# Attention in front of a mixture-of-experts stack: planes and first weights made inside attention's plan, tilings of TensorE grouped, memory matrices loaded in four batches

## Chip, cores and metric

The kernel runs on one core of one Trainium2 chip. The metric is the device time of one execution in microseconds (us); smaller is better. Values are the median of several executions, and one further execution was recorded by the hardware profiler.

## The reference

Attention over 4 batches, 8 heads, 576 positions, 64 channels, with a linear memory beside it; then a mixture of 8 experts with a balanced gate; then a feed-forward layer.

```python
scores = np.where(causal, -1e9, scale * q @ k.T); a = softmax(scores); local = a @ v
q_p = phi(q); mem_out = (q_p @ M_prev) / (q_p . z_prev + 1e-6)     # phi: elu + 1
x = g * mem_out + (1 - g) * local                                   # g: sigmoid of beta, per head
P = exp(x @ w_gate - max); 8 rounds: rows of P to 1, columns of P to N / E
x = sum over e of P[:, e] * (relu(x @ w1[e]) @ w2[e])               # 2304 x 512, hidden 1024
out = g2(x @ w_in) @ w_out                                          # hidden 2048
```

## The kernel before, in words

**Two plans.** The order of the work on every engine is written by a list scheduler (`Plan`). Each operation has a kind, an engine, an estimated cost and a priority; `Plan.order` walks through a simulated time, gives each free engine the ready operation with the smallest priority, and the instructions are issued in that order, so that every engine runs its own queue strictly in it. In the first plan (attention) the priority is the pair's number plus an offset of the operation's kind (`AHEAD`); in the second (experts and feed-forward) it is a due time alone. All operations of the first plan are issued ahead of all of the second.

**Attention** works on 16 pairs of heads (`pair(p)`, 4 pairs in a batch). SP loads q, k, v and z. TensorE turns q and k (`Tq0`, `Tq1`, `Tk0`, `Tk1`; `Tk1`, line 339, turns k's last 64 positions as a 64-row operand). ACT and DVE split them into a rounded high part and a low part. The scores `S0` to `S3` (line 411) use the array as two 64-row halves, one for each head, and `S4` (line 447) is full size. DVE takes the row minima (`mn`, line 415), ACT the exponentials (`ex`, line 421), POOL the scaling (`no`, line 470). TensorE turns the weights (`A0` to `A4`, line 291), ACT and DVE copy them (`at`, lines 491 and 504) into `bat`, of which there is one buffer. Then TensorE adds up in one PSUM buffer the memory's part `me` (lines 520 and 521, on `mblk`, the memory matrices of all 16 pairs), and the values' parts `av0` to `av3` (lines 532 and 534), two 64-column halves of the array, and `avt` (line 544), 64 by 64 quarters. `xh` copies the sum to `xa` (lines 556 to 561). The memory branch is `m0a` to `m0h`, `M1`, `qt`; its `m0b` (line 359) is a one-operation pass on POOL. `mblk` is filled by two DMAs (line 1002) that are issued when the fourth z load has been.

**The gate's logits** of finished batches (`g0`, line 892) are operations of the first plan for 13 of 18 blocks; the last 5 blocks and the eight rounds (`g1` to `g8`, lines 892 to 956) belong to the second.

**Experts and feed-forward** run in 60 units of about 31 us. A unit's first products (lines 802 to 804) take the planes of a superblock of 768 tokens: seven combinations of blocks of `xa`, each split into high and low (`add_planes`: `xt` on DVE, line 727; high on ACT, line 735; low on DVE, line 736), and w1's seven combinations (`add_weights`: `ws` on POOL, line 631; lines 642 and 644). The second products are lines 840 to 842. All 14 planes and the weights of the first unit are made by operations of the second plan.

Of the kernel before, what the change touches and what calls it, by code (L numbers as in the profile page):

```python
# [9 lines left out]
F32 = mybir.dt.float32  # L10
# [56 lines left out]
class Plan:  # L67
# [6 lines left out]
    AHEAD = {"ldq": -2.5, "ldk": -2.5, "ldv": 0.606644, "ldz": -0.0188182, "dupq": 2.5, "dupk": -1.11634, "Tq0": -0.582609, "Tq1": 0.34955, "Tk0": -0.348844, "Tk1": -0.811355, "Tt": -0.756224, "xqh": 1.14314, "xql": -1.02368, "kh": -2.48941, "kl": 2.5, "xqht": 0.447842, "kht": -2.5, "xqlt": -2.31585, "klt": -2.17001, "m0a": -2.28731, "m0b": 0.537231, "m0c": 0.387496, "m0d": 0.0204494, "m0e": 2.5, "m0f": -1.69614, "m0g": -2.5, "m0h": -2.5, "M1": 1.28311, "M1t": -2.5, "qt": 0.255714, "qtt": 0.106151, "S0": -2.5, "mn0": -0.618995, "ex0": -0.690281, "S1": 0.300177, "mn1": 0.479532, "ex1": 1.23372, "S2": 0.320698, "mn2": 1.81199, "ex2": -1.35932, "S3": -1.28738, "mn3": -1.07555, "ex3": 0.927263, "S4": -0.414386, "mn4": -0.748203, "ex4": 2.5, "rs0": -0.939336, "no0": -2.5, "no1": 1.07992, "no2": 1.36276, "no3": -1.05966, "no4": 1.36881, "A0": -0.654903, "at0": -1.24412, "A1": 0.733921, "at1": 0.715315, "A2": 1.22899, "at2": 2.07211, "A3": 0.131368, "at3": 1.10354, "A4": 1.48159, "at4": -1.63997, "A4t": -0.147975, "at4t": 2.5, "me": 1.67645, "av0": -1.11291, "av1": -0.469304, "av2": 0.199915, "av3": -0.505524, "avt": -0.468038, "xh": 0.600085, "xl": -1.65062, "g0": 1.02324, "g1": -0.814666, "g2": -1.20931, "g3": 0.801005}  # L74
# [36 lines left out]

    def prio(self, x):
        return (x.p if self.strict else x.p + self.AHEAD.get(x.kind, 0.0), x.n)

    def order(self):
# [9 lines left out]
        slots = {r: r.free for r in self.rings}  # L125
        if self.strict:
            self.queue()
        while len(out) < len(self.ops):
            if not events:
                raise RuntimeError(str([(round(x.p), x.kind, [(b.ring.name, b.slot, b.may(x)) for b in x.bufs]) for e in engines for x in sorted(todo[e], key=self.prio)[:6]]))  # L130
# [8 lines left out]
            for e in engines:  # L139
# [19 lines left out]
                x.start = t  # L159
                free[e] = t + x.cost  # L160
# [4 lines left out]
                for y in x.then:  # L165
                    y.wait -= 1
                    y.ready = max(y.ready, t + x.cost + (x.lat or (self.LATENCY[e] if y.eng != e else 0.13 if e == "DVE" else 0.033)))
                    if not y.wait:
                        todo[y.eng].append(y)
                        heapq.heappush(events, y.ready)  # L170
        self.length = max(free.values())
# [4 lines left out]
def tile_attn_moe_ffn(  # L176
# [53 lines left out]

    att = ExitStack()
# [10 lines left out]
    qe = acon.tile([P, 2, P], F32, name="qe")  # L242
    mblk = acon.tile([P, B * NPAIR, P], F32, name="mblk")
# [18 lines left out]
    r_ke = ring(qk, [TAIL, 2, D], F32, "ke", 2)  # L262
# [30 lines left out]
    def pair(p):  # L293
# [5 lines left out]
        for nm, buf, src in (("q", bq, q), ("k", bk, k), ("v", bv, v)):  # L299
# [7 lines left out]
            if nm == "k":  # L307
                o("ld" + nm, "SP", 0.18, lambda s_=s_: nc.sync.dma_start(
                    out=bke(), in_=s_[:, SM:S, :].rearrange("h s d -> s h d")), wr=[(bke, 0)])
# [21 lines left out]
        for nm, buf, e_, ps in (("q", bq, bqe, bpq), ("k", bk, bke, bpk)):  # L331
# [3 lines left out]
            def turn_tail(e_=e_, ps=ps, nm=nm):  # L335
                if nm == "q":
                    transposes(ps()[:, SM:], [e_()])
                else:
# [3 lines left out]
            o(f"T{nm}1", "PE", 0.15, turn_tail, rd=[(e_, 0)] + ([(e_, 1)] if nm == "q" else []), wr=[(ps, 1)])  # L342
        mq, tq = slice(0, SM), slice(SM, S)
        whole = [(bpq, 0), (bpq, 1)]
        o("xqh", "ACT", 0.6, lambda: nc.scalar.activation(bqh(), bpq()[:, 0 : SM + P], AF.Copy, scale=-SCALE),
          rd=whole, wr=[(bqh, 0)])
        o("xql", "DVE", 0.75, lambda: nc.vector.scalar_tensor_tensor(
# [3 lines left out]
        o("kh", "ACT", 0.55, lambda: nc.scalar.copy(bkh(), bpk()[:, 0:S]), rd=whole, wr=[(bkh, 0)])  # L351
        o("kl", "DVE", 0.68, lambda: nc.vector.tensor_tensor(
# [5 lines left out]
        o("m0a", "ACT", 0.57, lambda: nc.scalar.activation(be(), bq(), AF.Exp), rd=raw, wr=[(be, 0)])  # L358
        o("m0b", "POOL", 0.68, lambda: nc.gpsimd.tensor_scalar(
            out=be(), in0=be(), scalar1=1.0, scalar2=None, op0=ALU.min), wr=[(be, 0)])  # L360
        o("m0c", "DVE", 0.8, lambda: nc.vector.scalar_tensor_tensor(
# [11 lines left out]
        o("m0d", "POOL", 1.51, zmul, rd=[(bqp, 0), (bzr, 0), (bzt, 0)], wr=[(be, 0)])  # L373
        o("m0e", "DVE", 0.67, lambda: nc.vector.tensor_reduce(out=br(), in_=be(), axis=AX.X, op=ALU.add),
          rd=[(be, 0)], wr=[(br, 0)])
        o("m0f", "DVE", 0.08, lambda: nc.vector.scalar_tensor_tensor(
            out=br(), in0=br(), scalar=1e-6, in1=d9[:, hp, :], op0=ALU.add, op1=ALU.mult), wr=[(br, 0)])
        o("m0g", "DVE", 0.13, lambda: nc.vector.reciprocal(out=br(), in_=br()), wr=[(br, 0)])
# [8 lines left out]
        o("m0h", "POOL", 1.33, scale_phi, rd=[(br, 0)], wr=[(bqp, 0)])  # L387
# [7 lines left out]
        o("qt", "ACT", 0.48, lambda: nc.scalar.copy(bqt()[:, mq], pm()[:, 0:SM]), rd=[(pm, 0)], wr=[(bqt, 0)])  # L395
# [563 lines left out]
    with tc.manual_schedule():  # L959
# [25 lines left out]
        for p in range(NP):  # L985
            pair(p)
# [9 lines left out]
        for n, x in enumerate(order):  # L996
# [10 lines left out]
            if n == free:  # L1007
                early.close()
# [74 lines left out]
```

## Time and profile before

| | us |
|---|---|
| median of 3 executions | 2176.34 (2176.3 to 2178.87) |
| profiled execution | 2174.11 |
| its span, first to last instruction | 2172.3 |

The page gives for each engine the busy time, and the work that ended last. Windows give the same for stretches of time; their columns are start and end, length, busy time and instructions of PE, PEld, DVE, ACT and POOL, the granted clock of TensorE as a share of 2.4 GHz (1.00 is 2.4 GHz, 0.50 is 1.2 GHz), the DMA engines' busy share, and GB/s. A timeline lists instructions of one engine in order: start, length, line and operation, and in brackets the idle time before it and what ended it; neighbouring ones of one kind stand in one line with their count. A group by shape has, behind its count, the busy time, the mean of one in ns, and the idle time before them. On TensorE instructions overlap, so that what a line takes is read from its start to the start of the next line.

### The profile page before, as it was taken

Reading aid. Unit: us, or ns where it says so; the run is one execution under the profiler, and the core shown is the slowest. Engines: PE = TensorE matmul, PEld = TensorE weight load, DVE = VectorE, ACT = ScalarE, POOL = GpSimd, SP = SyncE. Lnnn points to the kernel's source line nnn. Section 1 sums busy time; section 2 is a strip of 40 time slices with the busy share of each in tenths; the row PEclk is TensorE's granted clock in tenths of the full one; section 3 lists DMA queues with packets and bytes.
Section 4 is the critical chain, followed back from the end, with each engine's and each line's share of the span. In section 5 each row is a group of like instructions: output and inputs, shape, how many; then the busy total and the mean of one; then the engine's idle time right before and its main releaser. Section 6 shows DMA issues by size and latency. Waiting matters only on the chain.

```text
span 2172.3 us, 31537 instructions
## 1 busy us (share of the span) xinstructions
PE 2141.2 (99%) x11163; PEld 1875.6 (86%) x11163; DVE 1579.1 (73%) x2882; ACT 1135.9 (52%) x2785; POOL 903.3 (42%) x967
## 2 busy tenths in 40 slices
PE   6999989999999999999999999999999999999999
PEld 4666689989898989999898989899999989898988
DVE  5766599887865688887655588885555587898985
ACT  5776554444444554444444454444444456777773
POOL 4867454443433334343433343343334334344340
PEclk8999989999999999999999999999999999999999
DMA  4323123332322223333222223322212212122211
GB/s 94 81 65 70 45 68 97 107 112 97 95 86 69 69 75 110 106 111 90 83 69 69 68 83 97 103 87 69 77 59 68 68 62 75 56 100 73 98 64 39
DMA packets 165054, 174.56 MB, mean 80 GB/s; under 512 B 70432, under 2 KB 121632, under 8 KB 164896
## 3 DMA queue, kind: packets, MB, share of 16 engines
q1 hardware_dynamic: 164752, 172.54, 26.4%
q8 instruction: 88, 1.44, 0.3%
q14 instruction: 70, 0.57, 0.1%
q10 hardware_dynamic: 144, 0.00, 0.0%
HBM read 159.40 MB, written 13.11 MB: 79 GB/s over the span
## 4 chain that ended last, share of the span: by engine, by line
PE 97%; DVE 1%; DMA 1%; SPq 1%; issue 0%; POOL 0%; ACT 0%; DVEq 0%; POOLq 0%
PE py L841 15%; PE py L842 15%; PE py L840 15%; PE ph L804 13%; PE ph L803 13%; PE ph L802 13%; PE s L291 4%; PE s L534 2%; PE s L411 2%; PE s L447 1%; PE s L521 1%; PE s L892 1%; PE pk L882 0%; PE pk L892 0%; PE s L520 0%
## 5 line engine op out<-in xcount | busy, mean ns | idle before, releaser
L644 POOL TENSOR_TENSOR w1l<-ws,w1h 128x512 fp32r<-128x512 f32 x240 | 326.9, 1380 | 1022.2 <-ACT w1h L642 1022.1
L804 PE MATMUL ph<-xh,w1l 128*128 128x384 f32 x1680 | 568.0, 338 | 1.5 <-POOL w1l L644 1.5
L803 PE MATMUL ph<-xl,w1h 128*128 128x384 f32 x1680 | 567.7, 338 | 0.0
L802 PE MATMUL ph<-xh,w1h 128*128 128x384 f32 x1680 | 564.9, 336 | 0.6 <-ACT pt L783 0.6
L842 PE MATMUL py<-w2h,hl 128*128 128x512 f32 x1440 | 565.4, 393 | 0.0
L841 PE MATMUL py<-w2l,hh 128*128 128x512 f32 x1440 | 565.0, 392 | 0.0
L840 PE MATMUL py<-w2h,hh 128*128 128x512 f32 x1440 | 562.2, 390 | 0.0
L783 ACT COPY pt<-ph 128x384 f32<-128x384 f32 x480 | 230.1, 480 | 541.4 <-PE ph L804 495.4
L788 DVE TENSOR_TENSOR hx<-ph,pt 128x384 f32<-128x384 f32 x480 | 264.1, 553 | 217.7 <-PE ph L804 121.3
L802 PEld LDWEIGHTS ph<-xh,w1h 128*128 128x128 f32 x1680 | 316.4, 188 | 21.1 <-ACT pt L783 1.1
L803 PEld LDWEIGHTS ph<-xl,w1h 128*128 128x128 f32 x1680 | 315.9, 188 | 20.0
L842 PEld LDWEIGHTS py<-w2h,hl 128*128 128x128 f32 x1440 | 270.0, 187 | 57.3
L804 PEld LDWEIGHTS ph<-xh,w1l 128*128 128x128 f32 x1680 | 316.4, 188 | 2.3 <-POOL w1l L644 2.0
L841 PEld LDWEIGHTS py<-w2l,hh 128*128 128x128 f32 x1440 | 270.3, 188 | 40.7
L840 PEld LDWEIGHTS py<-w2h,hh 128*128 128x128 f32 x1440 | 270.5, 188 | 40.1
L762 ACT ACTIVATE hh<-hx 128x384 fp32r<-128x384 f32 x384 | 192.7, 525 | 196.5 <-DVE hx L788 196.2
L866 DVE SCALAR_TENSOR_TENSOR xa<-py,pg,xa 128x512 f32<-128x512 f32 x264 | 191.4, 748 | 131.0 <-PE py L842 129.1
L763 DVE SCALAR_TENSOR_TENSOR hl<-hx,hh 128x384 fp32r<-128x384 f32 x384 | 218.5, 588 | 74.3 <-ACT hh L762 72.3
L631 POOL TENSOR_TENSOR ws<-wr 128x256 f32<-128x256 f32 x240 | 199.8, 853 | 100.7 <-DMA wr<-in_moe_w_dram 87.1
L642 ACT CAST w1h<-wr 128x256 fp32r<-128x256 f32 x360 | 132.9, 403 | 89.2 <-PE ph L803 88.8
L661 DVE TENSOR_TENSOR w2l<-wr,w2h 128x512 fp32r<-128x512 f32 x240 | 165.3, 723 | 5.3 <-ACT w2h L660 5.3
L642 ACT CAST w1h<-ws 128x256 fp32r<-128x256 f32 x480 | 162.8, 405 | 0.0
(143 smaller groups left out, 2330.5 us busy)
## 6 DMA issues: line engine op xcount, KB each, us to landing
wr<-in_moe_w_dram SPq DMA_DIRECT2D x192, 512.0 KB, 3.6
wr<-wk SPq DMA_DIRECT2D x48, 512.0 KB, 3.3
cr<-in_moe_w_in_dram SPq DMA_DIRECT2D x16, 512.0 KB
wk<-xt SPq DMA_DIRECT2D x32, 256.0 KB, 4.6
cr<-in_moe_w_out_dram SPq DMA_DIRECT2D x16, 512.0 KB
out_dram<-xa SPq DMA_DIRECT2D x18, 256.0 KB, 2.0
q<-in_q_dram SPq DMA_DIRECT2D x32, 128.0 KB, 2.7
k<-in_k_dram SPq DMA_DIRECT2D x32, 128.0 KB, 2.9
```

The costliest lines, as they stand in the source:

```text
L631: o(p, "ws", "POOL", 0.8, lambda: nc.gpsimd.tensor_tensor(out=st()[:, k], in0=in0(), in1=in1(), op=op), [(raw, 0)] + [(st, i) for i in rd] ...
L642: o(p, "w1h", "ACT", 0.42, lambda k=k: nc.scalar.copy(hi()[:, k], x(k)), rd, [(hi, k)])
L644: o(p, "w1l", "DVE" if eng is nc.vector else "POOL", cost, lambda: eng.tensor_tensor(out=lo()[:, i:j], in0=x(slice(i, j)), in1=f32(hi()[:, ...
L763: o(p, "hl", "DVE", 0.75, lambda: nc.vector.scalar_tensor_tensor(out=r(), in0=x(), scalar=0.0, in1=f32(a()), op0=ALU.max, op1=ALU.subtract ...
L783: o(p, "pt", "ACT", 0.49, lambda t=part[name], s=bank[b]: nc.scalar.copy(t(), s()[:, :TH]), [(bank[b], 0)], [(part[name], 0)])
L788: o(p, "hx", "DVE", 0.56, lambda s=bank[b], t=part[name]: nc.vector.tensor_tensor(out=x(), in0=s()[:, :TH], in1=t(), op=ALU.add), [(bank[b ...
L802: nc.tensor.matmul(out_, lhsT=wh, rhs=xhi()[:, kk], start=fresh and kk == 0, stop=False, **more)
L803: nc.tensor.matmul(out_, lhsT=wh, rhs=xlo()[:, kk], start=False, stop=False, **more)
L804: nc.tensor.matmul(out_, lhsT=wl, rhs=xhi()[:, kk], start=False, stop=kk == 1, **more)
L840: nc.tensor.matmul(py(), lhsT=a()[:, ts_], rhs=hi()[:, j, :], start=f == 0, stop=False)
L841: nc.tensor.matmul(py(), lhsT=a()[:, ts_], rhs=lo()[:, j, :], start=False, stop=False)
L842: nc.tensor.matmul(py(), lhsT=r()[:, ts_], rhs=hi()[:, j, :], start=False, stop=f == 3)
```

## The change

- Priorities and costs of the first plan are new numbers throughout. The plan now adds 0.1 us on TensorE where the tiling differs from that of the operation before (`TILING`, `CHANGE`).
- `Tk1` turns a zero-padded 128 x 128 tile (`ke`) at full size. `S0` and `S1` are one operation into one PSUM buffer. `av0` to `av3` and `avt` are one operation, which waits for all copies of the turned weights. An `A` operation now holds `bat`, so that it is not planned before the pair ahead has let go of it.
- `m0b` gets a second operation (times 1). `at1` goes from ACT to DVE in odd pairs.
- `mblk` is loaded in four batches of two DMAs, one batch behind each of the first four z loads.
- The planes of the first superblock and w1 of the first unit's first half are operations of the first plan, with a priority behind that of pair 15 (before its kinds' offsets). Their high parts are made on POOL instead of ACT. The planes wait for the first 8 pairs; the weights' load waits for the last use of q's and k's buffers, where their memory is.
- The pools of the second plan are opened in two steps for that; w1's two buffers lie in two pools.

```diff
+    TILING = {"S0": 1, "S1": 1, "S2": 1, "S3": 1, "av0": 2, ..., "avt": 3}
+    CHANGE, SAME = 0.1, 0.0
...
-                    nc.tensor.transpose(ps()[:, SM:S], e_().rearrange("p h d -> p (h d)"), ident[0:TAIL, 0:TAIL])
+                transposes(ps()[:, SM:], [e_()])
...
-            out=be(), in0=be(), scalar1=1.0, scalar2=None, op0=ALU.min), wr=[(be, 0)])
+            out=be(), in0=be(), scalar1=1.0, scalar2=1.0, op0=ALU.min, op1=ALU.mult), wr=[(be, 0)])
...
+            ps, c = (first, 2 * P * i) if i < 2 else (r_s.new(), 0)
+            if i != 1:
+                def rows_of(ps=ps, i=i, w=w):
+                    for j, c, n in ((0, 0, 2 * P), (1, 2 * P, 2 * P)) if i == 0 else ((i, 0, w),):
+                        scores([halves(ps())[:, h, c : c + n] for h in range(2)], slice(P * j, P * (j + 1)), 0, n)
...
-                  rd=[(ba[i], h)], wr=[(pt, h)])
+                  rd=[(ba[i], h)], wr=[(pt, h), (bat, 8 + 2 * i + h)])
...
-            o(f"av{j}", "PE", [1.02, 0.78, 0.56, 0.35][j], local,
-              rd=vs + [(bat, i) for i in range(j, NQ + 1)], wr=[(bpo, 0)])
+        o("av0", "PE", 2.86, all_local,
+          rd=vs + [(bat, i) for i in range(NQ + 1)] + [(bat4, 0), (bat4, 1)], wr=[(bpo, 0)])
...
+                    o(p, "bh", "POOL", 0.7, lambda k=k: copy1(v4(hi())[:, k], x()[:, k]), xk + rd, [(hi, k)])
...
+        def low(p, *a, **k):
+            return op(NP - 0.5 + 0.01 * p, *a, **k)
+        early_rings = (r_q, r_k, r_qh, r_ql, r_kh, r_kl)
+        add_planes(low, 0, 0, [(keys[p], 0) for p in range(NPAIR * -(-SB // S))])
+        add_weights(low, 0, 0, 1, 0, [x for x in plan.ops if any(b.ring in early_rings for b in x.bufs)])
...
-                if nz == 4:
+                if nz <= B:
                     for h in range(2):
+                        r = slice(D * h, D * (h + 1))
                         nc.sync.dma_start(
-                            out=mblk[D * h : D * (h + 1), :, D * h : D * (h + 1)],
-                            in_=M_prev.rearrange("b (hp h) d e -> h d (b hp) e", h=2)[h],
+                            out=mblk[r, NPAIR * (nz - 1) : NPAIR * nz, r],
+                            in_=M_prev[nz - 1].rearrange("(hp h) d e -> h d hp e", h=2)[h],
...
-        add_planes(o, 0, 0)
-        for g in range(2):
-            add_weights(o, 0, g, 1, GROUP * 2 * g)
+        add_weights(o, 0, 1, 1, GROUP * 2)
```

## Rows read from the trace of the kernel before

**Rows 1.** The page, part 1: busy time, share of the span, instructions.

```profile
PE 2141.2 (99%) x11163; PEld 1875.6 (86%) x11163; DVE 1579.1 (73%) x2882; ACT 1135.9 (52%) x2785; POOL 903.3 (42%) x967
```

**Rows 2.** Windows of a stall, a pair, attention's end and the rest.

```profile
40.00:47.00 7.00, 3.40 (x11) 2.31 (x11) 0.46 (x1) 0.00 (x0) 0.00 (x0) 0.53 0.47 90
104.80:118.30 13.50, 13.50 (x99) 8.78 (x98) 9.93 (x32) 10.57 (x28) 10.82 (x16) 1.00 0.34 77
265.50:293.30 27.80, 20.99 (x98) 18.90 (x96) 23.39 (x48) 16.52 (x43) 14.98 (x12) 0.69 0.12 39
293.30:2172.30 1879.00, 1875.29 (x9398) 1694.14 (x9397) 1389.42 (x2317) 947.86 (x2295) 714.62 (x704) 1.00 0.26 82
```

**Rows 3.** Waits of PE, whole span: total, times, longest.

```profile
PE s L520 <- DMA mblk<-in_M_prev_dram: 8.7, 1, 8.7
PE pk L949 <- DVE cs L947: 2.6, 1, 2.6
```

**Rows 4.** Timelines of SP, DVE and ACT between 38 and 48.

```profile
38.49 1.35 SPq L1002 DMA_DIRECT2D mblk<-in_M_prev_dram  x2
...
46.54 0.96 DVE L491 COPY at<-s 128x768 f32<-128x768 f32 x1 [10.12 <-PE s L291]
...
47.08 0.59 ACT L504 COPY at<-s 128x512 f32<-128x512 f32 x1 [10.76 <-PE s L291]
```

**Rows 5.** Timeline of PE, 104.5 to 118.6, one pair's period.

```profile
105.30 0.50 PE L411 MATMUL s<-kh,qh 64*128 64x512 f32 x2
105.64 0.40 PE L411 MATMUL s<-kl,qh 64*128 64x512 f32 x2
105.88 0.39 PE L411 MATMUL s<-kh,ql 64*128 64x512 f32 x2
106.20 0.66 PE L291 MATMUL s<-ident,a 128*128 128x128 f32 x4
...
111.33 0.60 PE L291 MATMUL s<-ident,k 128*128 128x128 f32 x4
111.76 0.27 PE L291 MATMUL s<-ident,qe 128*128 128x128 f32 x1
111.97 0.27 PE L339 MATMUL s<-ident,ke 64*128 64x64 f32 x1
112.17 0.49 PE L520 MATMUL s<-qt,mblk 128*128 128x128 f32 x2
...
115.16 0.97 PE L534 MATMUL s<-at,v 128*64 128x448 f32 x4
116.07 0.33 PE L291 MATMUL s<-ident,qp 128*128 128x128 f32 x1
116.32 0.76 PE L534 MATMUL s<-at,v 128*64 128x320 f32 x4
117.01 0.39 PE L411 MATMUL s<-kh,qh 64*128 64x256 f32 x2
```

**Rows 6.** POOL's groups, 104.8 to 118.3; the last row is the page's.

```profile
L359 POOL TENSOR_SCALAR e<-e 128x576 f32<-128x576 f32 x1 | 1.6, 1648 | 0.0
L470 POOL TENSOR_SCALAR a<-a,rs,o 128x384 f32<-128x384 f32 x2 | 1.3, 662 | 0.0
...
L644 POOL TENSOR_TENSOR w1l<-ws,w1h 128x512 fp32r<-128x512 f32 x240 | 326.9, 1380 | 1022.2 <-ACT w1h L642 1022.1
```

**Rows 7.** Timeline of PE: the gate's two longest runs, ahead of and behind attention's end.

```profile
141.62 3.74 PE L892 MATMUL s<-gw_raw,xa 128*128 128x8 f32 x32
...
266.37 6.84 PE L892 MATMUL pk<-gw_raw,xa 128*128 128x8 f32 x40 [0.83 <-ACT xa L559]
```

**Rows 8.** Window behind the third run of logits, same columns as group 2.

```profile
254.80:261.60 6.80, 6.80 (x33) 6.80 (x34) 0.58 (x2) 2.09 (x3) 3.96 (x7) 0.50 0.00 1
```

**Rows 9.** Groups by shape, DVE, 262 to 290: busy, mean ns, idle.

```profile
L727 DVE TENSOR_TENSOR xt<-xa,xt 128x384 f32<-128x384 f32 x4 | 3.8, 998 | 0.0
L727 DVE TENSOR_TENSOR xt<-xa 128x384 f32<-128x384 f32 x4 | 2.1, 550 | 0.0
```

More of the change, by code (lines that the diff above doesn't have):

```diff
@@ L110, in queue @@
                     line.append(b)
+    TILING = {"S0": 1, "S1": 1, "S2": 1, "S3": 1, "av0": 2, "av1": 2, "av2": 2, "av3": 2, "avt": 3}
+    CHANGE, SAME = 0.1, 0.0
     def prio(self, x):
-        return (x.p if self.strict else x.p + self.AHEAD.get(x.kind, 0.0), x.n)
+        same = x.eng == "PE" and self.TILING.get(x.kind, 0) == self.tiling
+        return (x.p if self.strict else x.p + self.AHEAD.get(x.kind, 0.0) - self.SAME * same, x.n)
     def order(self):
@@ L125, in order @@
         slots = {r: r.free for r in self.rings}
+        self.tiling = 0
         if self.strict:
@@ L159, in order @@
                 x.start = t
+                if e == "PE":
+                    x.cost += self.CHANGE * (self.TILING.get(x.kind, 0) != self.tiling)
+                    self.tiling = self.TILING.get(x.kind, 0)
                 free[e] = t + x.cost
@@ L170, in order @@
                         heapq.heappush(events, y.ready)
+        for _, _, x in ends:
+            for b in x.bufs:
+                b.left -= 1
         self.length = max(free.values())
@@ L261, in tile_attn_moe_ffn @@
     r_qe = Ring(lambda: qe[:, next(turns_) % 2], 2)
-    r_ke = ring(qk, [TAIL, 2, D], F32, "ke", 2)
+    tails_ = iter(range(2 * NP))
+    r_ke = Ring(lambda: ke[:, next(tails_) % 2], 2)
     r_v = ring(io, [P, NG, D], F32, "v", 3)
@@ L460, in recip @@
                 nc.vector.reciprocal(out=x, in_=x)
-            o(f"rs{g0}", "DVE", 0.3, recip, rd=[(bsm, g) for g in range(g0, g1)], wr=[(brs, g0)])
+            o(f"rs{g0}", "DVE", 0.6, recip, rd=[(bsm, g) for g in range(g0, g1)], wr=[(brs, g0)])
         for j in range(NQ + 1):
@@ L494, in pair @@
             both_ = slice(0, 2)
-            if i == 2:
-                o(f"at{i}", "DVE", (2 * n * P + 62) * 1.042e-3, lambda move=move: move(nc.vector.tensor_copy, both_),
+            if i == 2 or i == 1 and p % 2:
+                o(f"at{i}", "DVE", 0.96 if i == 2 else 0.7, lambda move=move: move(nc.vector.tensor_copy, both_),
                   rd=[(pt, 0), (pt, 1)], wr=[(bat, i)])
             else:
-                o(f"at{i}", "ACT", 2 * n * P * 0.833e-3 + 0.06, lambda move=move: move(nc.scalar.copy, both_),
+                o(f"at{i}", "ACT", (0.37, 0.59, 0.8, 1.0)[i], lambda move=move: move(nc.scalar.copy, both_),
                   rd=[(pt, 0), (pt, 1)], wr=[(bat, i)])
@@ L721, in add_planes @@
         v4 = lambda t: t.rearrange("p k (i t) -> p k i t", t=P)
-        xk = [(kx[i0 + i], 0) for i in range(2 * HT)]
+        xk0 = [(kx[i0 + i], 0) for i in range(2 * HT)]
+        xk = xk or xk0
         def tmp(in0, in1, op, rd, p):
@@ L986, in tile_attn_moe_ffn, with open_pool @@
             pair(p)
+        def open_pool(name):
+            bufs = {"s": 2, "ph": 4, "py": 3}.get(name, 1)
+            space = {"d": bass.MemoryType.DRAM, "ph": PSUM, "py": PSUM, "pk": PSUM}.get(name)
+            more = {} if space is None else dict(space=space)
+            if space is not bass.MemoryType.DRAM:
+                more["reuse_waits"] = "tile"
+            pools[name] = ctx.enter_context(tc.tile_pool(name=f"m_{name}", bufs=bufs, **more))
         for j in range(B - 1):
```

113 lines of the change are left out of this document (60 added, 53 removed).

## Prediction

> **What bounds the kernel now.** I read the page's busy times first, then windows by stage, then the waits of PE, then the timelines of the stretches that stood out. PE is busy for 99% of the span [rows 1], which says little by itself: matmuls overlap, and the same work takes twice as long where the clock is granted at 0.50. The windows say more [rows 2]. From 293.30 to the end PE has 1875.29 us of work in 1879.00 us at clock 1.00. None of that work changes, so these 1879 us stay. What can move is the 293 us ahead of them, in three places. The start has a stall: PE waited 8.7 us, in one piece, for `mblk` [rows 3]. The middle is dense: a pair takes 13.50 us and PE is busy for 13.50 of them at clock 1.00, while POOL has 10.82, ACT 10.57 and DVE 9.93 [rows 2]. Attention's end is thin: 27.80 us at a mean clock of 0.69 [rows 2].
>
> **First change: the memory matrices in batches.** The two `mblk` DMAs were issued at 38.49 and took 1.35 us of SP [rows 4]. DVE then stood idle for 10.12 us and ACT for 10.76 us [rows 4], and POOL did nothing from 40 to 47 [rows 2]. So all three had run as far ahead as they could, and nothing else is late next: without this wait all of them move up. The clock was also low there: 0.53 from 40 to 47, of which PE worked 3.40 us [rows 2], or 1.7 us at the full clock. The first batch goes out behind the first z load, and `me` of pair 0 needs no other. Gain: at most 8.7 + 1.7 = 10.4. Against it, eight DMAs instead of two: at 1.35 / 2 = 0.68 us each [rows 4], six more hold SP 4.1 us longer at the start, and the loads of pairs 1 to 3 are queued behind them, with TensorE's turns waiting for those. If all of it counts, 6.3 are left. A first pair that is late for another reason would leave none of it. I take 9, nearer the upper end, because the engines idled through the whole wait; range 0 to 10.4.
>
> **Second change: fewer tilings.** In the pair from 104.8 to 118.3 I count 16 changes of tiling on PE: three visits to the scores' row halves, one of `Tk1`, four of `av`, one of `avt`. A change is priced by what it adds to neighbours of the same shape. Four turns in a row take 111.76 - 111.33 = 0.43, so 0.11 each; a single turn between two tilings takes 116.32 - 116.07 = 0.25 [rows 5]. That is 0.14 on the neighbour's side of a visit. The visit itself adds more: `av` takes 0.91 for 448 columns (115.16 to 116.07) and 0.69 for 320 (116.32 to 117.01) [rows 5]. The slope is 0.22 for 128 columns, which leaves 0.91 - 448 x 0.00172 = 0.14 that doesn't depend on columns. So each `av` visit that goes is worth 0.14 to 0.28. Four of five go: 0.56 to 1.12. I take 0.8, the middle, because part of the fixed 0.14 may be loads of new weights that stay. `Tk1`: the turn ahead of it takes 111.97 - 111.76 = 0.21, itself 0.20 [rows 5], and at full size both would take 0.11; `me` behind it pays again. That is 0.2 to 0.3; I take 0.25. A visit of the scores: S3's takes 106.20 - 105.30 = 0.90, its steps in stream 0.24 (105.64 to 105.88), three of them 0.72, so 0.18, and 0.14 beside it: 0.32 [rows 5]. There are three visits now, and the merged S0 and S1 allow three or fewer. The gain is 0 to 0.65; I take 0.15, near the lower end, because `SAME` is 0 and nothing but the new priorities brings the visits together. Sum for a pair: 0.8 + 0.25 + 0.15 = 1.2 (0.76 to 2.07). From the end of the stall, 47, to 265.5 there are 218.5 us. In them lie 104 matmuls of the gate's logits, by my count, at 3.74 / 32 = 0.117 each [rows 7], 12.2 us, and some 7 us that the clock at 0.50 beside them costs; 199 us are left, 14.5 pairs. 1.2 x 14.5 = 17.4. A period of 12.3 is nearer to the other engines' times, so some waits of PE come back. I take off 2.4 and keep 15, range 4 to 28.
>
> That cover has to hold. POOL's one-operation pass takes 1648 ns on 576 columns, a two-operation one 662 ns on 384 [rows 6], so at most about 1.0 on 576, and POOL falls from 10.82 to about 10.2. `at1` has 512 columns, 0.59 on ACT, and some 0.7 on DVE, where 768 take 0.96 [rows 4]; in every other pair it changes over, which leaves ACT at 10.3 and DVE at 10.3. The merged `av` waits for `avt`'s copies too, and while PE runs it (some 3 us) the turns and scores of the next pair are queued behind it, with ACT and DVE behind those; they have work of the pairs on either side. I cost that at nothing; if their cover is gone, it is inside the 2.4.
>
> **Third change: planes and first weights inside attention.** Behind attention's last `avt` PE needs: 40 logits matmuls, which took 6.84 where the clock was mostly 0.50 and would take 3.74 x 40 / 32 = 4.7 at the full clock [rows 7]; 48 products of 384 columns until 293.3, by my count, at 0.18 each where 512 columns take 0.24 [rows 5], 8.6; about 0.5 for the rounds. That is 13.8 of 27.8 [rows 2], so 14 are lost: half clock and waits for planes, weights and rounds. With planes and weights ready, products follow the logits at once. What stays: 0.83 until `xa` is there, 6.84 - 4.7 = 2.1 for the slow logits [rows 7], 1 to 3 until the dense products have the clock back (half of 2 to 6 us; a slow stretch here lasts 6.8 [rows 8]), and waits for the rounds of 0 to 2.6, which is what one such wait cost [rows 3]. That is 4 to 8.6, so the gain is 5.4 to 10. I take 8.
>
> What is moved costs other engines work in the second half of attention. DVE: 8 `xt` and 14 low parts of 550 ns [rows 9], 12.1 us. POOL: 14 high parts at the 662 ns of the same width [rows 6], 9.3, and of the first weights two low parts at 1380 [rows 6] and four combinations of half that width, about 5.5. ACT: seven casts of 256 columns, about 3 by 0.59 for 512 [rows 4]. Over the last 8 pairs POOL gets 14.8 / 8 = 1.9 more for each: 10.2 + 1.9 = 12.1 beside PE's 12.3. At that load it is hidden, but barely. It has priority behind pair 15 before offsets, so what doesn't fit waits for the gaps that the gate's logits leave.
>
> Two engines on one memory show too: `xt` with two inputs took 550 ns while POOL was idle and 998 ns on average while POOL was at work [rows 9]. The Trainium skill (GPSIMD Engine Reference, section 1, Specifications) says that POOL shares its SBUF interface with VectorE and that DVE instructions with two SBUF inputs contend with it. By this, high parts on POOL beside low parts on DVE would take nearly twice as long.
>
> **Sum.** 9 + 15 + 8 = 32. The profiled execution, 2174.11 with a span of 2172.3 and 1.8 around it, would become 2142. It lies 2.2 below the median of 2176.34; I take the difference from the median: 2144. The ends of the terms give 0 + 4 + 5.4 = 9.4 (2167) and 10.4 + 28 + 10 = 48.4 (2128).
>
> **Rivals.** *Another engine bounds the pairs.* POOL at 12.1, slowed by DVE at its side, holds the second half of attention at 13.5. For: the sum above, and 998 against 550 ns [rows 9]. Against: POOL is idle beside the gate's logits, and all its added work can wait. Then only the first 6.5 pairs gain: 9 + 7.8 + 8 = 25, 2151; if the whole of attention stays at 13.5, 2159. *The change does not do what it says at one end.* Either batches queue up in front of q and k, so that the first pair is as late as now (32 - 9, 2153), or low-priority planes are left over at attention's end, so that the thin stretch stays (32 - 8, 2152). For: the planes come last in the order, and SP issues almost without pause at the start. Against: `mblk` is 5 us behind everything else, and half of attention is time enough for 12 us of DVE. *Slower: the clock falls inside the pairs.* With the scores together and `av` in one run, what is left between them is long runs of turns alone. Where PE ran the rest of some logits and then turns (254.80 to 261.60), it was busy for 6.80 of 6.80 and the clock stood at 0.50 [rows 8]. Each us at 0.50 loses half a us. Half such a stretch in each pair, 3.4, costs 1.7 x 14.5 = 25: 2169. A whole one costs 49: 2193. It turns the sign once 32 x 2 = 64 us, or 4.4 us of each pair, run at 0.50. Against: a pair already has runs of turns and is at 1.00 throughout [rows 2]. The Trainium skill (TensorE: Matmul & The Clock Gate, Part 4) says that transposes don't count as busy for the clock in the way that matmuls do; by that rule this is what grouping would bring, and the trace agrees with it only where logits stood beside the turns.
>
> **How the numbers follow.** The forecast, all three terms at about these sizes: 0.60, at 2144, with 2128 to 2160 of its own. Another engine as bound: 0.16, at 2151 to 2159. One end that doesn't gain: 0.10, at about 2152. The clock inside the pairs: 0.09, a third of it near 2169, a third near now, a third slower. Something that I don't see: 0.05, most of it slower. The range of 2127 to 2163 holds the forecast nearly whole and the next two, and leaves out the clock's cases and the tails. About 0.2% (4.4 us) is what a measurement of this kernel can tell from no change. Faster by more: 0.60 + 0.16 + 0.10 + 0.03 = 0.89; within it 0.03 + 0.01 = 0.04; slower 0.03 + 0.04 = 0.07.
>
> **What would show it.** Right: no wait of PE for `mblk` over 1 us, and the first `avt` near 43 instead of 52.7; some 8 to 10 tiling changes in a pair, and a period near 12.3 with PE dense at 1.00; products right behind the last logits, and the dense stage beginning about 19 us after the last `avt` instead of 28. Wrong: PE waits for POOL or ACT inside pairs, clock 0.50 away from the logits, `xt` still running on DVE behind attention, or a dense stage that is longer than 1879.

## The result, and the profile after

The changed kernel takes 2141.42 us (median of 4 runs, 2140.47 to 2144.26) against 2176.32 (4 runs), a ratio of 0.9841 with a 95% interval of 0.9824 to 0.9858. Its profiled execution took 2140.47, with a span of 2138.7; the span is 33.6 shorter than that of before, 2172.3. The forecast was 2144, so the total and the sign came out. The three terms behind the total did so less well: two were too small, and the first was too large. What the first one named, the batches, brought nothing that shows in the new order (e3 below). That the total is so close is in part luck.

To see this, the span is cut at marks that all the kernels have: the `avt` of the first, the second and the last pair, read from PE's timelines. At the first `avt` both kernels have the same work behind them: 173 matmuls in the trace of after, 174 in that of before. At the second they have not (264 and 250), because the two orders divide the pairs differently. So before and after are compared from the first `avt`. The experiments that keep the order of after can be compared with it from the second one, too. The column "at 0.50" adds up the stretches between the second and the last `avt` in which the granted clock was 0.50; about half of it is the time that this cost, since PE is busy there. The kernels e1 to e12 are the experiments below; their marks are those of one execution each.

| kernel | median us | first `avt` at | second `avt` at | from there to the last `avt` | of it at 0.50 | last `avt` to the end |
|---|---|---|---|---|---|---|
| before | 2176.32 | 52.7 | 63.3 | 201.9 | 13.7 | 1907.1 |
| after | 2141.42 | 47.6 | 60.5 | 181.5 | 10.2 | 1896.7 |
| e1 tile_pad | 2156.42 | 48.5 | 62.2 | 195.8 | 17.1 | 1898.3 |
| e2 tile_mix | 2169.21 | 49.3 | 63.8 | 204.9 | 13.7 | 1899.9 |
| e3 mblk_one | 2143.15 | 46.5 | 59.0 | 183.3 | 10.2 | 1899.6 |
| e4 both_late | 2149.13 | 47.0 | 61.1 | 182.6 | 17.1 | 1905.3 |
| e5 old_batches | 2172.17 | 44.9 | 58.0 | 204.6 | 20.5 | 1909.4 |
| e6 planes_late | 2149.45 | 47.2 | 61.3 | 182.7 | 17.1 | 1903.5 |
| e7 pool_twice | 2166.03 | 50.1 | 64.9 | 201.1 | 20.5 | 1898.2 |
| e8 start_pool_one | 2145.20 | 49.2 | 62.0 | 184.9 | 17.1 | 1896.5 |
| e9 k_first | 2163.08 | 46.6 | 61.8 | 201.5 | 23.9 | 1898.2 |
| e10 k_first_pool_one | 2158.51 | 45.8 | 61.0 | 199.0 | 20.5 | 1896.7 |
| e11 k_all | 2171.59 | 60.4 | 75.3 | 197.0 | 17.1 | 1896.6 |
| e12 pool_one | 2142.51 | 47.4 | 60.2 | 188.0 | 23.9 | 1896.7 |

From before to after: -5.1 up to the first `avt`, -18.1 over the 15 pairs from there to the last one, -10.4 from the last `avt` on. Forecast were -9, -15 and -8. In neither kernel does time at 0.50 lie between the first and the second `avt`.

The kernel before was timed again beside the experiments. Its medians were 2178.22 beside e1 to e4, 2177.27 beside e5 to e8, 2179.42 beside e9 to e11 and 2178.34 beside e12. So a difference of 1 to 3 us between a run and after, which was timed beside a median of 2176.32, says nothing by itself.

The page's busy time (part 1) of after stands beside [rows 1]: PE has 27.4 us less at the same count of instructions, so most of the gain is matmuls that take less time, not waits that went. Not all of that is tilings: in these two executions the clock was at 0.50 for 47.8 us of before and 28.4 us of after.

```profile
PE 2113.8 (99%) x11163; PEld 1876.2 (88%) x11163; DVE 1578.7 (74%) x2891; ACT 1125.7 (53%) x2763; POOL 917.6 (43%) x981
```

Windows of after, columns as in [rows 2]: the stretch of the old stall, two pairs one after the other, a run of turns inside a pair, attention's end up to the 48th product, and the rest.

```profile
40.00:47.00 7.00, 6.71 (x52) 4.43 (x54) 6.13 (x26) 6.41 (x20) 6.89 (x10) 1.00 0.40 85
...
85.40:97.60 12.20, 12.20 (x101) 8.96 (x99) 9.78 (x31) 10.14 (x27) 10.00 (x14) 1.00 0.40 92
97.60:109.90 12.30, 12.30 (x100) 9.04 (x98) 11.04 (x33) 10.65 (x29) 12.00 (x17) 1.00 0.34 78
113.86:116.63 2.77, 2.77 (x26) 2.60 (x25) 2.61 (x8) 2.40 (x6) 2.22 (x2) 1.00 0.40 97
242.00:259.90 17.90, 16.56 (x102) 15.56 (x101) 8.78 (x19) 8.87 (x23) 8.41 (x10) 0.90 0.31 108
259.90:2138.66 1878.76, 1874.83 (x9397) 1693.89 (x9396) 1386.71 (x2324) 946.67 (x2293) 714.30 (x705) 1.00 0.26 82
```

Beside [rows 2]: a pair takes 12.2 to 12.3 in place of 13.5, PE dense in both. Attention's end takes 17.90 at 0.90 in place of 27.80 at 0.69. The rest is 1878.76 against 1879.00: the same, as it should be. The old stall's stretch is full of work. What is not seen there is where the stall went. The waits of PE in after, beside [rows 3] (total, times, longest):

```profile
PE s L305 <- DMA k<-in_k_dram: 7.7, 2, 6.5
PE s L305 <- DMA q<-in_q_dram: 5.2, 2, 4.5
PE s L305 <- POOL a L485: 4.6, 3, 3.9
PE py L877 <- DVE hl L798: 1.3, 1, 1.3
```

The wait of 8.7 for `mblk` is gone, and two others, 6.5 for `k` and 3.9 for POOL's `a`, stand ahead of the first pair. PE's timeline shows them, and where the first pair's memory product now lies (L535):

```profile
23.90 1.08 PE L305 MATMUL s<-ident,k 128*128 128x128 f32 x4 [6.50 <-DMA k<-in_k_dram]
...
32.54 0.91 PE L305 MATMUL s<-ident,a 128*128 128x128 f32 x2 [3.88 <-POOL a L485]
...
43.66 0.39 PE L535 MATMUL s<-qt,mblk 128*128 128x128 f32 x2
...
44.84 0.45 PE L548 MATMUL s<-at,v 128*64 128x128 f32 x4
45.11 2.54 PE L550 MATMUL s<-at,v 128*64 128x448 f32 x16
47.58 0.33 PE L565 MATMUL s<-at,v 64*64 64x64 f32 x4
```

The product starts at 43.66. In the kernel before it started at 43.60, released by the load.

### The profile page after: what moved, and what is told of

It reads as the page before. It is cut to its first block, busy times and chain, and to the rows that moved or that the text cites. A ratio compares the mean times of both kernels' runs of the same rounds, so it can differ in the third digit from the quotient of the medians.

```text
span 2138.7 us, 31548 instructions
## 1 busy us (share of the span) xinstructions
PE 2113.8 (99%) x11163; PEld 1876.2 (88%) x11163; DVE 1578.7 (74%) x2891; ACT 1125.7 (53%) x2763; POOL 917.6 (43%) x981
## 4 chain that ended last, share of the span: by engine, by line
PE 97%; DVE 1%; SPq 1%; POOL 1%; issue 0%; DMA 0%; ACT 0%; DVEq 0%; POOLq 0%; ACTq 0%
PE py L876 16%; PE py L877 15%; PE py L875 15%; PE ph L839 14%; PE ph L838 14%; PE ph L837 14%; PE s L305 3%; PE s L550 2%; PE s L422 2%; PE s L927 1%; PE s L536 1%; PE s L462 1%; PE pk L917 0%; POOL a L485 0%; SPq L316 0%
## 5 line engine op out<-in xcount | busy, mean ns | idle before, releaser
L797 ACT ACTIVATE hh<-hx 128x384 fp32r<-128x384 f32 x384 | 192.8, 525 | 188.2 <-DVE hx L823 188.0
L662 POOL TENSOR_TENSOR ws<-wr 128x256 f32<-128x256 f32 x240 | 199.0, 850 | 100.7 <-DMA wr<-in_moe_w_dram 87.0
```

The source lines that it names most:

```text
L662: o(p, "ws", "POOL", 0.8, lambda: nc.gpsimd.tensor_tensor(out=st()[:, k], in0=in0(), in1=in1(), op=op), [(raw, 0)] + [(st, i) for i in rd] ...
```

## Experiments

### Is the tiling change itself what a pair saves?

A pair of before has 16 changes of tiling, one of after 7. The visits of `av` shrink from four to one, and two of the three visits of the scores now lie next to `av` or `avt`. PE's timeline of after, the seven lines of one pair at which the tiling changes:

```profile
110.20 0.39 PE L422 MATMUL s<-kh,qh 64*128 64x256 f32 x2
...
111.11 1.97 PE L305 MATMUL s<-ident,a 128*128 128x128 f32 x16
...
116.63 0.50 PE L422 MATMUL s<-kh,qh 64*128 64x512 f32 x2
...
117.53 0.49 PE L535 MATMUL s<-qt,mblk 128*128 128x128 f32 x2
...
118.70 0.44 PE L422 MATMUL s<-kh,qh 64*128 64x384 f32 x2
...
119.42 0.45 PE L548 MATMUL s<-at,v 128*64 128x128 f32 x4
...
122.16 0.33 PE L565 MATMUL s<-at,v 64*64 64x64 f32 x4
```

Two kernels put changes back while the work stays equal. Both add four small full-size products in each pair, which add products with zeros. e1 has them in one place, ahead of `av`; e2 has one behind each product of `av`. They differ in the number of changes alone: 116 against 215 in all of attention, where after has 103 and before 255. (e1 has 13 more than after, because its full-size products part the scores from `av`; "no tiling changes" in its expectation is not quite so.)

```
 def all_local():                        # e1
+    for f in locals_:
+        nc.tensor.matmul(bpo()[:, c0 + P : c0 + P + 8], lhsT=mask[:, 0:P], rhs=ident[:, 0:8], start=False, stop=False)
     for f in locals_:
         f()

 def all_local():                        # e2
     for f in locals_:
         f()
+        nc.tensor.matmul(bpo()[:, c0 + P : c0 + P + 8], lhsT=mask[:, 0:P], rhs=ident[:, 0:8], start=False, stop=False)
```

> The changed kernel with four small extra matmuls (full-size weights of zeros, 8 columns, added to the sum) in every pair, all four ahead of the values' first product, so that no tiling changes. Each is two passes like the gate's logits, 0.117 a pass: 4 x 0.23 = 0.94 us for a pair, 15 us for 16 pairs. Both theories: 2141 + 15 = 2156.

> The same four extra matmuls, one behind each of the values' four products, so that four visits to the half tiling stand where one was; the order of everything else is the same. Theory (a change of tiling costs PE time by itself): over the kernel with the four in front, 4 visits x 0.25 to 0.28 = 1.0 to 1.1 us for a pair, 16 to 18 in all: about 2173. Rival (the pairs became shorter by the new order and costs, not by tilings): the same as with the four in front, 2156.

Measured: 2156.42 and 2169.21. The 99 changes cost 12.8 us, 0.13 each. The stretch between the marks says the same: with half of the time at 0.50 taken off, 195.8 - 8.5 = 187.3 and 204.9 - 6.8 = 198.1, so 10.8 for the 86 changes that lie there, 0.13. PE's timeline of one pair of e2:

```profile
115.61 0.93 PE L550 MATMUL s<-at,v 128*64 128x448 f32 x4
116.47 0.39 PE L559 MATMUL s<-ident,mask 128*128 128x8 f32 x2
116.78 0.97 PE L550 MATMUL s<-at,v 128*64 128x448 f32 x4
```

A small product holds PE for 0.31 here (116.47 to 116.78), and `av`'s product ahead of it for 0.86 (115.61 to 116.47). In e1 the four small ones stand in one row of eight that takes 1.06, 0.26 for two. So only a part of a change is seen on the small one, and the rest on its neighbour. 9 changes fewer in a pair at 0.13 give 1.2, and the period fell by 1.25. The expectation for e2 was too high by its count: it added four visits of 0.25 to 0.28 to a pair, where the edit adds three (from one to four). Two changes at 0.13 are 0.26, so the price of a visit was right. That the changes would be free is ruled out. The Trainium skill (TensorEngine Tiling (Array Packing), Tiling Modes, Key Properties) says that a switch of the tiling mode drains TensorE. It gives no price; these two runs do.

### Were the batches worth 9?

e3 is the kernel after with one load of all memory matrices behind the fourth z load, where before had it. e5 is the kernel before with the batches and nothing else.

```
-                if nz <= B:                    # e3
-                    ... mblk[r, NPAIR * (nz - 1) : NPAIR * nz, r] <- M_prev[nz - 1]
+                if nz == B:
+                    ... mblk[D * h : D * (h + 1), :, D * h : D * (h + 1)] <- M_prev
```

> The changed kernel with the memory matrices loaded at once behind the fourth z load, as before; all else and its order unchanged. Theory A (in the new order the first product with them stands no earlier on PE than before, at 43.7 us, and waits for nothing): the one load is issued at about 37 to 38 and lands by 42 to 43, PE waits under 1 us for it, and the time is 2141 within 2. Rival, as predicted (the batches are what took the wait away): PE waits 4 to 8 us for it and the time is 2145 to 2150.

> The kernel before with one thing of the change: the memory matrices in four batches, one behind each of the first four z loads. Theory A (in the old order PE stood still for that load alone, as the prediction has it): the wait of 8.7 us goes, the first avt comes 8 to 10 us earlier, 2166 to 2169. Theory B (the next thing in the queues, a load that SP issues later because of the batches, takes its place as it did in the changed kernel): 2 to 5 us, 2171 to 2174.

e3 took 2143.15 (2139.84 to 2144.15), 1.7 more than after, with the runs of both overlapping. Its second `avt` even came sooner, at 59.0. In the new order PE gets to the product at 42.47, and the one load has landed by then. It gave that back: 1.8 were lost between the second and the last `avt` and 2.9 behind the last `avt`, where 10.2 us at 0.50 stood in place of 3.4, and its span is 3.2 longer than after's. Against the kernel before that was timed beside it e3 is 35.1 faster, and after is 34.9 faster against its own. So in the new order the batches bring nothing that these runs can show.

In the old order they do: e5 took 2172.17 (10 runs) against 2177.27, a ratio of 0.9974 (0.9964 to 0.9983), about 5 us. PE's timeline of e5 shows the product at 33.92 without a wait, and the first `avt` at 44.94, where before had it at 52.66:

```profile
33.92 0.44 PE L520 MATMUL s<-qt,mblk 128*128 128x128 f32 x2
...
44.94 0.48 PE L544 MATMUL s<-at,v 64*64 64x64 f32 x4
```

So 7.7 were gained at the first `avt`, which is close to the 9. But the second `avt` came only 5.4 sooner (57.97 against 63.34): in the kernel before the second pair followed the first by 10.7, in e5 by 13.0. PE runs the same matmuls in the same order in both, without a pause. What differs is the clock. The windows from the first to the second `avt`, first of before, then of e5, columns as in [rows 2]:

```profile
52.66:63.34 10.68, 10.68 (x78) 6.67 (x77) 7.33 (x17) 6.12 (x14) 10.15 (x14) 1.00 0.39 87
```

```profile
44.94:57.97 13.03, 13.03 (x77) 8.61 (x77) 6.39 (x17) 6.43 (x15) 11.19 (x15) 0.80 0.38 84
```

In e5 the granted clock stood at 0.50 from 43.37 to 50.19. Of that, 5.2 us lie behind the first `avt`; half of them is 2.6, and the pair took 2.4 longer. In before the stretch at 0.50 lay from 39.75 to 46.58, where PE mostly waited and worked for 2.98 us, so that it cost some 1.5 there. Behind the second `avt`, e5 met more time at 0.50 than before (20.5 against 13.7, so 3.4 us lost) and lost 2.3 more from the last `avt` on, where its last logits took 7.40 in place of 6.84 and another 3.4 us stood at 0.50. In its profiled execution, 2173.85, nearly all of the start's gain had gone by the end; the median keeps 5.

### What holds the start in the new order?

In after, SP issued `v`, z and the first batch ahead of the `k` for which PE waited until 23.90. SP's timeline of after:

```profile
15.26 0.58 SPq L330 DMA_DIRECT2D zr<-in_z_prev_dram  x1
15.89 1.11 SPq L335 DMA_DIRECT2D zt<-in_z_prev_dram  x2
17.04 1.29 SPq L1053 DMA_DIRECT2D mblk<-in_M_prev_dram  x2
18.38 1.15 SPq L316 DMA_DIRECT2D v<-in_v_dram  x2
19.57 0.56 SPq L319 DMA_DIRECT2D v<-in_v_dram  x1
20.23 0.96 SPq L316 DMA_DIRECT2D k<-in_k_dram  x2
```

Three kernels take things out of its way. e8 moves the memory matrices to ACT's queue at the very start (and has the minimum pass with one operation, for which see below). e9 gives the `k` loads of pairs 1 and 2 a sooner due time, e11 those of all pairs.

```
+        for h in range(2):                     # e8, ahead of the pairs; the batches behind ldz are gone
+            r = slice(D * h, D * (h + 1))
+            nc.scalar.dma_start(out=mblk[r, :, r], in_=M_prev.rearrange("b (hp h) d e -> h d (b hp) e", h=2)[h])
-    "ldk": 1.065                               # e9, used for k of pairs 1 and 2
+    "ldk": 1.065, "ldk0": 0.3
-    "ldk": 1.065                               # e11
+    "ldk": -0.9
```

> The changed kernel with two edits that leave the order as it is: the memory matrices in two DMAs on ACT's queue ahead of the first pair (SP has nothing of them), and POOL's minimum pass with one operation again (1.65 us instead of 2.13). Theory: at the start PE waits for k's third load 4 instead of 6.5 us and for POOL's scaling some 3.4 instead of 3.9; the first avt at about 45 instead of 47.6; 2138 to 2140. Rival (the start's gain is given back where TensorE's clock falls behind the logits, at another place in each order): 2141 within 2.

> The kernel after, with the k loads of pairs 1 and 2 ahead of v and z in SP's order: k of pair 2 is then issued some 5 us sooner than at 20.23. Theory A (what kept the batches' gain from coming through is SP's queue: v, z and the first batch stood ahead of a k that PE's order needs next): PE's wait of 6.5 for k at 23.90 falls to at most 2, first avt from 47.6 to 43-44, time 2137 to 2139 (4 less, of which logits at the low clock can give back 2). Rival B (the start is bound by the chain behind PE: passes, sums and weights of pair 0 on DVE, ACT and POOL): the wait moves from k to POOL's a, which now holds 3.9, first avt stays at 46.5 or later, time 2140 to 2143.

> The kernel after, with k loads 2 pairs sooner in the order for all pairs (offset -0.9 in place of 1.065), nearer to the kernel before (-2.5). The start then has k first in all its pairs. Theory A (k's place in SP's queue is what the start lost): PE's wait for k falls under 2, first avt 42 to 45, time 2137 to 2140, and nothing of k shows later, where SP has slack. Rival B (SP's queue only moves the wait: q, v and z come later): other waits for DMA of 2 us or more at the start, time 2140 or more.

All three are slower than after: 2145.20, 2163.08 and 2171.59. e8's 3.8 is little more than the noise. For the start, e9 decides against the queue. SP issued the third `k` at 15.34, PE's wait for it fell to 1.27, and the first `avt` came at 46.6, where after had 47.6. PE's timeline of e9 shows what was late next, DVE's `kl` and POOL's `a`:

```profile
18.72 0.63 PE L305 MATMUL s<-ident,k 128*128 128x128 f32 x4 [1.27 <-DMA k<-in_k_dram]
23.98 0.39 PE L422 MATMUL s<-kh,qh 64*128 64x256 f32 x2 [2.97 <-DVE kl L363]
...
31.21 2.20 PE L305 MATMUL s<-ident,a 128*128 128x128 f32 x6 [3.54 <-POOL a L485]
```

e8 agrees: its wait for `k` was still 3.7 with no `mblk` on SP at all, PE now waited for `kh` (2.05) and `kl` (1.29), and the second `avt` came at 62.0, later than after's 60.5. So, as far as these two runs show, several chains end together ahead of the first pair in this order, and taking one away uncovers the next.

In e11 the start itself grew worse. PE's waits for `k` came to 12.6, the longest 5.6, and the second `avt` was at 75.3. Of the 12.6, 4.4 are for the very first load, where after waits 4.5 for `q`. The longest is for a fifth `k`, which SP issued at 24.95, behind z, a batch and `v`, and which PE's own new order asks for at 28.79. The clock costs about as much: it stood at 0.50 from 21.5 to 55.6, and PE was busy for 21.69 of these 34.1 us, which by half costs 10.8.

The 21.7 us that e9 lost, and half of e11's 30.2, lie elsewhere, and I had not expected them. A due time changes the order that the planner makes for everything behind it. In e9 the pairs behind the second took 19.6 and 15.4 before they settled at 12.3. Its window from 61.80 to 81.40:

```profile
61.80:81.40 19.60, 15.79 (x103) 11.51 (x101) 12.52 (x36) 11.46 (x31) 16.26 (x18) 0.83 0.30 68
```

PE was idle for 3.8 of 19.6 there and part of it ran at 0.50. Between the marks e9 met 23.9 us at 0.50 in place of 10.2, which is 6.8 of the 20.0 that it lost there. So e9 and e11 answer the question on the start, and their totals say nothing about `k`: they show how much hangs on the set of due times as a whole.

### Planes and weights: which of the two?

e4 makes both where before made them, in the second plan; e6 only the planes.

```
-        add_planes(low, 0, 0, [...])                    # e4 and e6
-        add_weights(low, 0, 0, 1, 0, [...])             # e4
+        add_planes(o, 0, 0)                             # e4 and e6, in the second plan
+        add_weights(o, 0, 0, 1, 0)                      # e4
```

> The changed kernel with the first superblock's planes and the first unit's first weights back in the second plan (high parts on ACT). Theory: the thin stretch behind attention comes back, 8 to 10 us; from the last avt to the 85th product of the experts 36 us instead of 27; 2150 to 2151. Rival (another wait behind attention, the gate's rounds or slow clock, would have cost as much anyway): under 3 us, 2141 to 2144.

> The changed kernel with the planes alone back in the second plan; the first weights stay in the first. Theory: the planes (22 DVE operations of 0.55 to 1.0 us behind attention) are the larger part: PE waits for low parts on DVE, 6 to 8 us, 2147 to 2149. Rival: the weights are the larger part (POOL's combinations and low parts), then under 3 us, 2142 to 2144.

2149.13 and 2149.45: 7.7 and 8.0 more than after. By the table, from the last `avt` to the end takes 1905.3 and 1903.5 in place of 1896.7, which is 8.6 for both and 6.8 for the planes alone. The 1.8 between them does not show in the medians, so what the early weights bring by themselves is not shown. The waits of PE say why both are slower, first e4's, then e6's:

```profile
PE ph L838 <- DVE xl L771: 3.0, 1, 3.0
PE pk L984 <- DVE cs L982: 1.7, 1, 1.7
```

```profile
PE pk L984 <- DVE cs L982: 5.2, 2, 4.5
```

With the planes late, DVE makes low parts while the gate's rounds (`cs`) need it too, and PE, which works in order, stands at one or the other. With weights early and planes late (e6), the wait moved nearly whole to `cs`. Waits are not all of it: behind the last `avt` e4 has 13.7 us at 0.50, e6 10.2 and after 3.4. PE was busy for 8.9 us of that in e4, 8.2 in e6 and all 3.4 in after, so that the clock costs the two some 2.4 to 2.8 more, and the longer waits the rest.

The table also has the price of the early work inside attention. With the time at 0.50 taken off, the 14 pairs take 174.1 and 174.2 in e4 and e6 and 176.4 in after. So some 2.3 us of the early planes are not hidden.

### How much slack has POOL?

e7 has the minimum pass twice, with the same values as one. e12 has it with one operation, as before had. e10 is e9 with one operation.

```
-    tensor_scalar(..., scalar1=1.0, scalar2=1.0, op0=ALU.min, op1=ALU.mult)
+    tensor_scalar(..., scalar1=1.0, scalar2=None, op0=ALU.min)          # e8, e10, e12
+    for _ in range(2): tensor_scalar(..., op0=ALU.min, op1=ALU.mult)    # e7
```

> The changed kernel with POOL's minimum pass made twice in each pair (same result), 2.13 us more on POOL; the order is unchanged. POOL now has 10.0 and 12.0 us in alternate pairs of 12.25. Theory (POOL is next behind PE, with about 1 us to spare on average): the mean goes to 13.1 and the pairs' period with it, 0.9 x 12 = about 11 us, PE waits for POOL's scaling: 2150 to 2154. Rival (the buffers hide it): period stays 12.25, under 3 us.

> As the run with k of pairs 1 and 2 first, and the minimum pass on POOL with one operation as in the kernel before: 0.48 us less of POOL in each pair (2.13 to 1.65). Theory A (PE bounds a pair at 12.25, POOL's 12.0 in every other pair is just inside): period stays 12.2 to 12.3, time within 1 us of the run with k first alone. Rival B (POOL's last half us still costs PE in the crowded second half of attention, where the early planes and weights lie): 2 to 4 us less than that run.

> The kernel after, with one edit: the minimum pass on POOL has one operation as in the kernel before (1.65 us in place of 2.13 by the profiles), in the same order. Theory A (PE bounds a pair, and POOL's 12.0 beside 12.25 is just inside): pairs stay at 12.2 to 12.3, time 2139 to 2143. Rival B (POOL costs PE in the second half of attention, where 0.48 us in each pair decide, as it was worth 4.6 us where k came first): period of pairs 8 to 14 shorter, 2135 to 2138.

POOL's groups by shape, first of after, then of e12 (its row has the shortest, median and longest duration in ns, then the first and last start), beside [rows 6]:

```profile
L370 POOL TENSOR_SCALAR e<-e 128x576 f32<-128x576 f32 x16 | 34.1, 2134 | 6.6 <-ACT e L369 6.6
L485 POOL TENSOR_SCALAR a<-a,rs,o 128x512 f32<-128x512 f32 x32 | 26.4, 833 | 0.0
```

```profile
L370 POOL TENSOR_SCALAR e<-e x16: 1644/1648/1662, 5.7 to 197.9; 128x576 f32<-128x576 f32 x16
```

The form with two operations takes 2.13, not less than 1.65 but more. It costs nothing all the same: e12 took 2142.51 (2139.29 to 2146.69), and its pairs without the time at 0.50 take 176.0 against 176.4.

e7 took 2166.03, which is 24.6 more than after for a pass of 2.13; 2150 to 2154 was expected. Its pairs take about 14.1 and 13.3 in turn, and POOL is busy for 13.94 of 14.20 and 12.94 of 13.20 in the two windows shown. By the table, 4.4 of the loss lie ahead of the second `avt`, 14.5 in the pairs without the time at 0.50, 5.1 are that time and 1.5 lie behind the last `avt`. So the theory's 11 for the pairs was near, and it had left out the start and the clock. The windows and the wait of PE (lines lie three later in this kernel):

```profile
64.90:79.10 14.20, 13.38 (x100) 8.91 (x98) 9.22 (x25) 8.87 (x22) 13.94 (x16) 1.00 0.29 66
...
93.20:106.40 13.20, 12.88 (x100) 8.90 (x98) 9.17 (x25) 8.71 (x22) 12.94 (x15) 1.00 0.32 73
```

```profile
PE s L305 <- POOL a L488: 14.3, 17, 6.1
```

So POOL is the next bound, just behind PE: 12.00 of 12.30 in every other pair of after. Less work on it brings nothing (e12). More costs what goes beyond the slack and somewhat over it; that the wait also falls on turns that PE can't overtake may be why, but no run shows it. e10 was 4.6 faster than e9, which looked like the rival's answer. By the table it is not: of the 4.8 between their spans 0.8 lie ahead of the second `avt`, 1.7 are the clock between the marks and 1.5 lie behind the last `avt`, where e9 had 6.8 us at 0.50 and e10 3.4. That leaves 0.8 for POOL.

### What the clock does with equal code

e12 has the same order as after, and its pairs take the same time once the clock is counted. Yet the span of its profiled execution was 2144.9, 6.2 longer. Behind logits it met three stretches at 0.50, of which the first fence has the second and third; after met the two of the second fence:

```profile
212.51:222.75 10.24, 10.24 (x51) 8.45 (x51) 5.68 (x19) 1.33 (x4) 7.76 (x13) 0.50 0.00 0
233.00:239.80 6.80, 6.80 (x26) 4.26 (x27) 2.10 (x6) 1.50 (x4) 6.31 (x11) 0.50 0.40 134
```

```profile
215.84:219.25 3.41, 3.41 (x20) 2.63 (x20) 1.76 (x9) 0.41 (x1) 3.32 (x5) 0.50 0.00 0
164.63:171.46 6.83, 6.83 (x32) 6.54 (x32) 3.50 (x8) 2.13 (x8) 6.74 (x8) 0.50 0.00 0
```

23.9 against 10.2 at 0.50 is 6.8 lost, and 6.2 was measured. e8's 4.7 of span over after is 3.4 from the clock and 1.5 from the start in the same way. It is the execution and not the kernel that differs: another execution of e12 took 2139.29 at a mean clock of 0.994, the profiled one 2146.69 at 0.990. A few us either way in this kernel are thus the clock behind the logits, and a change of start time by one or two us can't be read from a total.

## Why the prediction came out, point by point

**First term, batches: forecast -9, measured -5.1 by the first `avt`, and none of it by the batches.** The step that failed is "nothing else is late next: without this wait all of them move up" [rows 2 to 4]. In the old order it held: e5 gained 7.7 at the first `avt`. But the change brought a new order along, in which PE waits for `k` and `a` ahead of the first pair and reaches the memory product at 43.66, as late as before. There the load is no longer what is late: without batches (e3) the first `avt` even came 1.1 sooner. The rival "batches queue up in front of q and k" holds in part: with the batches out of SP's queue there the longest wait for `k` was 4.2 (e3) and 3.7 (e8) in place of 6.5. The rest of the wait belongs to the new order. What makes the 5.1 was not isolated; 16 changes of tiling fewer ahead of the first `avt` (12 for 28) would be 2.1 at 0.13. The mark named for the term, a first `avt` near 43, was wrong: 47.6. "No wait for `mblk`" was right and proved little.

**Second term, tilings: forecast -15, measured -18.1, of which 1.7 is the clock.** The price of a pair, 1.2, was right against 1.25 [rows 5], and e1 and e2 show that the changes themselves are the cause. The count was 7 a pair, below the 8 to 10 that I named. From the first `avt` to the last there are 136 changes fewer (90 for 226), 17.7 us at 0.13. Measured without the clock are 16.4, and 18.7 with the 2.3 that the early planes cost there (e4). What failed is the deduction of 2.4 "so some waits of PE come back": behind the second `avt` no wait of PE is over 0.4 up to the last one. Three small figures are off as well: 199 / 13.5 is 14.7 pairs, not 14.5; 0.76 x 14.5 - 2.4 is 8.6, and how the lower end came to 4 is not worked out; and seven casts of 256 columns at half of 0.59 are 2.1 and not 3. They don't change the forecast by more than 0.3.

**Third term, planes and weights: forecast -8, measured -10.4 in all.** Products follow the logits at once, as claimed. PE's timeline of after, beside the second row of [rows 7]:

```profile
242.25 4.81 PE L927 MATMUL pk<-gw_raw,xa 128*128 128x8 f32 x40
246.91 0.67 PE L837 MATMUL ph<-xh,w1h 128*128 128x384 f32 x1
```

Two of the losses that I had let stay didn't: 0.83 for `xa`, and most of the slow logits, which took 4.81 in place of 6.84 because the clock was still up (0.96 from 242.25 to 246.91). e4 and e6 put 8.6 of the term on the early work, most of it on the planes. The rest, about 1.8, is near half of the difference in time at 0.50 behind the last `avt`: 17.1 us in before, 13.7 in e4. The dense stage began 17.9 behind the last `avt`; I had said 19.

**POOL and the pass.** "At most about 1.0 on 576" was wrong by a factor of two: 2.13. I had taken the price from a row of POOL with other operations on it, two multiplications [rows 6]. So POOL was at 10.00 and 12.00 in turn in pairs that had no plane yet, 11.0 on average, where I had put 10.2. The early planes found their room beside the gate's first logits. The window of after where they begin:

```profile
147.40:179.60 32.20, 31.80 (x232) 24.64 (x230) 25.00 (x74) 20.98 (x55) 30.27 (x39) 0.89 0.28 64
```

POOL is busy for 30.27 of 32.20 there, and PE idle for 0.40. That POOL hides "barely" was right, and e7 is the price of having less.

**The rivals.** *Another engine bounds the pairs* did not happen, by 0.3 us of POOL in every other pair. *The clock falls inside the pairs* did not happen either: 24 turns in a row ran at 1.00 (the window from 113.86 to 116.63 above), and in after the stretches at 0.50 lay at the start and behind logits alone. The Trainium skill (TensorE: Matmul & The Clock Gate, Part 4) says that transposes don't count as busy for the clock in the way that matmuls do; beside the dense pairs of this kernel nothing of that shows. Of the two inputs on DVE beside POOL [rows 9], the early `xt` took 0.56 and 0.65 on average, not 1.0, so the doubling that I had feared stayed away.

## What to carry to other kernels

Before a wait is counted as a gain, ask whether the new order still gets to that point sooner: undoing the batches in the finished kernel (e3) cost nothing, although in the old order they were worth 7.7 at the first pair. A wait can also lie over time at the low clock; with the wait gone, such time may fall on dense work, as in e5. Two orders are compared at a point where both have done the same work. When matmuls of different array tilings alternate, count the changes and price one from neighbouring rows; grouping them shortens a dense engine's work, and the next engine's busy time in the same period says how far that can go. An order made by a planner is one object: moving the due times of two pairs' `k` loads cost 21.7 us here, so judge each part of such a change by undoing it in the finished order.

## What the hardware showed that I had not expected

- POOL's one pass over 128x576 with a minimum took 1.65 us, with a minimum and a multiplication 2.13; two multiplications over 128x512 took 0.83.
- One change of the array's tiling between full size and the two column halves cost 0.13 us on PE, on average over 99 (e1 against e2; 86 of them between the marks give the same with the time at 0.50 taken off).
- The same matmuls of one pair, without a pause of PE, took 10.68 us at 1.00 and 13.03 where 5.2 us of them ran at 0.50 (before and e5).
- The same order of the same matmuls met 10.2 us at 0.50 in one execution and 23.9 in another (after and e12, which differ on POOL alone).
